# Attention with a fused feed-forward: the gated up products by one level of Strassen's scheme

## The chip, the cores and the metric

The kernel runs as one program on one core of a Trainium2 chip. Its time is the device time of one execution in microseconds; the kernel before takes 1141.07 us (median of three runs, 1141.06 to 1141.1). Five engines work side by side, each through its own instructions in order: TensorE (PE; its weight loads are listed apart as PEld), VectorE (DVE), ScalarE (ACT), GpSimd (POOL) and SyncE (SP), which here issues the DMAs. SBUF is the working memory, PSUM holds matmul results in eight banks per partition.

## The reference

Eight batches of eight heads attend over 576 positions with a learned relative bias; the result, 4608 tokens of 512 features, goes through a gated product and two further weight matrices:

```python
scores = scale * np.matmul(q, k.transpose(0, 1, 3, 2)) + bias      # (8, 8, 576, 576)
attn = softmax(scores)
x = np.matmul(attn, v).transpose(0, 2, 1, 3).reshape(4608, 512)    # tokens x features
a = x @ w1                       # w1, w2: 512 x 1024
b = x @ w2
h = a * b @ w3                   # (a * b) @ w3, w3: 1024 x 1024
out = h @ w_out                  # w_out: 1024 x 512
```

The four weight matrices arrive as 64-bit floats, so the kernel converts them on the chip.

## The kernel before, in words

There are three stages. **Attention** (to about 480 us) works through 32 units (head pair, batch) in an order that a table of times sets. It is the same in both kernels.

**Fold** (about 474 to 546 us of the profiled execution): w3 and w_out are multiplied into one 1024 x 512 matrix, since nothing stands between them. In 16 half steps, four 128-wide transposes go to PSUM (tile `w3t`), ACT and DVE split them into a high and a low part (`w3h`, `w3l`), and twelve matmuls accumulate into `wacc`. ACT and DVE then split each finished row block into two parts, which stand in the buffers `w3s`. Everywhere in the last two stages a 32-bit number is carried as a high part in the type fp32r, which PE takes at its fast rate, and a low part (the remainder, fp32r too); a product is three matmuls: high by high, low by high, high by low.

**Feed-forward** (from 546 us): nine chunks of 512 tokens, each with eight steps `ft` of 128 of the 1024 inner features. `up` makes the two products a and b of a step: for each of the two weight matrices, four blocks of 128 features times three matmuls, 24 matmuls of 512 columns into two PSUM tiles `up0`, `up1`. ACT copies `up0` (`a`), DVE multiplies (`g`), ACT and DVE split the product (`gh`, `gl`). `down` takes `gh`, `gl` as weights and the folded matrix as the moving operand: four token blocks times three matmuls, 12 matmuls of 512 columns into four PSUM tiles `o`. PE does the ups of step n+1 before the downs of step n, and `up0`, `up1` have two buffers each, so PE has a free bank to write while ACT and DVE read another. At a chunk's end ACT copies `o` to `osb` and SP stores it.

Two preparations run beside this. A weight piece (512 x 128 of w1 or w2) is fetched as 64-bit words by SP and narrowed (`narrow`: three operations of ACT, two of DVE, two of POOL), then split into `wh` (ACT) and `wl` (DVE); there are 16 pieces, one each 6.56 us by plan, beginning in the fold. The pieces of `ft` 0 and 1 lie in the pool `w01`, opened on the right side of SBUF, the other twelve in `wpool` on the left side. The chunk's x is loaded by SP, scaled by the softmax sums `rb` (DVE), and split (`xh` on POOL, `xl` on DVE).

The order of the work on PE, ACT, DVE and POOL is written out by hand: each step of a Python generator is entered in a list with a planned time (`put`), and `drive` emits them sorted by it. The planned times only set the order on each engine; when an instruction runs is settled by its waits. SP takes its DMAs in the order in which they are emitted.

Of the kernel before, what the change touches and what calls it, by code (L numbers as in the profile page):

```python
# [18 lines left out]
P = 128  # L19
# [64 lines left out]
def relpos_attention_moe(  # L84
# [29 lines left out]
    def f(ap):  # L114
        return ap.bitcast(F32)
# [401 lines left out]
    att_r.close()  # L517


    CH = 512  # L520
    NCH = NTOK // CH
    NT = CH // P
    STEP = 7.8
    moe = ctx.enter_context(ExitStack())
    w01 = moe.enter_context(tc.tile_pool(name="w01", bufs=1, side="right"))
    cv = moe.enter_context(tc.tile_pool(name="cv2", bufs=2, side="right"))

    ups = {}
    chunks = {c: dict(x=[None] * NC, g={}) for c in range(NCH)}

    def split_w(pool, t, m):
        src = (moe_w1, moe_w2)[m].rearrange("(c p) n -> p c n", p=P)[:, :, t * P:(t + 1) * P]
        w = cv.tile([P, NC * P], F32, name="w", bufs=3)
        for step in narrow(cv, src, NC * P, w, nc.sync, pieces=NC):
            step()
            yield
        w = w.rearrange("p (c n) -> p c n", c=NC)
        wh = pool.tile([P, NC, P], F32R, name=f"wh{m}{t}")
        nc.scalar.activation(wh, w, AF.Copy)
        yield  # L540
        wl = pool.tile([P, NC, P], F32R, name=f"wl{m}{t}")
        nc.vector.tensor_tensor(wl, w, f(wh), op=ALU.subtract)
        ups[m, t] = (wh, wl)

    def put_w(plan, pool, t, m, at):
        put(plan, split_w(pool, t, m), at - AT_W[0], *(at + d for d in AT_W[1:]))


    fo = ExitStack()
# [43 lines left out]
    def load_x(c):  # L593
        for cc in range(NC):
            xr = xs.tile([P, CH], F32, name=f"xr{cc}", bufs=1)
            nc.sync.dma_start(xr, x_d[cc][:, c * CH:(c + 1) * CH])
            rb = xs.tile([P, CH], F32, name=f"rb{cc}", bufs=1)
            for h, rows in enumerate((lo, hi)):
                load_r(rb, cc, rows, h, c * CH, (c + 1) * CH)
            chunks[c]["x"][cc] = (xr, rb)  # L600
        yield

    def split_x(c, cc):
        xr, rb = chunks[c]["x"][cc]
        nc.vector.tensor_tensor(xr, xr, rb, op=ALU.mult)  # L605
        yield
        xh = xs.tile([P, CH], F32R, name=f"xh{cc}")
        xl = xs.tile([P, CH], F32R, name=f"xl{cc}")
        nc.gpsimd.tensor_scalar(xh, xr, 1.0, 1.0, op0=ALU.mult, op1=ALU.mult)  # L609
        yield  # L610
        nc.vector.tensor_tensor(xl, xr, f(xh), op=ALU.subtract)
        chunks[c]["x"][cc] = (xh, xl)

    def up(c, ft):
        ps = []
        for m in range(2):
            acc = ps_ab.tile([P, CH], F32, name=f"up{m}")
            wh, wl = ups[m, ft]
            n = 0
            for cc in range(NC):  # L620
                xh, xl = chunks[c]["x"][cc]
                for l, r in ((wh, xh), (wl, xh), (wh, xl)):
                    nc.tensor.matmul(acc, l[:, cc], r, start=(n == 0), stop=(n == 3 * NC - 1))  # L623
                    n += 1
            ps.append(acc)
            yield
        a = gp.tile([P, CH], F32, name="a")
        nc.scalar.copy(a, ps[0])  # L628
        yield
        g = gp.tile([P, CH], F32, name="g")  # L630
        nc.vector.tensor_tensor(g, ps[1], a, op=ALU.mult)  # L631
        yield
        gh = gp.tile([P, CH], F32R, name="gh")
        nc.scalar.activation(gh, g, AF.Copy)  # L634
        yield
        gl = gp.tile([P, CH], F32R, name="gl")
        nc.vector.tensor_tensor(gl, g, f(gh), op=ALU.subtract)  # L637
        chunks[c]["g"][ft] = (gh, gl)

    def down(c, ft):  # L640
        d = chunks[c]
        gh, gl = d["g"].pop(ft)
        for t in range(NT):
            if ft == 0:
                d["o", t] = ps_o.tile([P, DO], F32, name=f"o{t}")
            sl = slice(t * P, (t + 1) * P)
            for n, (l, r) in enumerate(((gh, 0), (gh, 1), (gl, 0))):
                nc.tensor.matmul(  # L648
                    d["o", t], l[:, sl], folded[ft][:, r],
                    start=(ft == 0 and n == 0), stop=(ft == NF - 1 and n == 2),  # L650
                )
        yield
        if ft == NF - 1:
            for t in range(NT):
                o = op.tile([P, DO], F32, name="osb")
                nc.scalar.copy(o, d["o", t])
                nc.sync.dma_start(out[c * CH + t * P:c * CH + (t + 1) * P, :], o)
                yield


    for i in range(NF):
        put(later, split_wo(i), t_s + AT_WO + i * PACE_WO, t_s + AT_WO + i * PACE_WO + 0.8)
    for i in range(2 * NF):
        at = t_s + AT_F + min(i, N_F) * PACE_F0 + max(i - N_F, 0) * PACE_F
        put(later, fold(*divmod(i, 2)), *(at + d for d in AT_FOLD))
    for t in range(2):
        for m in range(2):
            put_w(later, w01, t, m, t_s + AT_W1 + PACE_W * (2 * t + m))
    drive([e for e in later if e[0] <= end])
    later = [e for e in later if e[0] > end]  # L670
    att.close()
    xs = moe.enter_context(tc.tile_pool(name="xs", bufs=2))
    wpool = moe.enter_context(tc.tile_pool(name="wpool", bufs=1))
    ps_ab = moe.enter_context(tc.tile_pool(name="ps_ab", bufs=2, space=PSUM))
    plan, t_f = [], t_s + AT_F + N_F * PACE_F0 + (2 * NF - N_F) * PACE_F + AT_FOLD[3]
    for n in range(4, 2 * NF):
        at = t_s + AT_W1 + PACE_W * n
        put_w(later if at < t_f - 10.0 else plan, wpool, n // 2, n % 2, at)
    put(later, load_x(0), end + 0.5)
    for cc in range(NC):  # L680
        put(later, split_x(0, cc), *(t_s + AT_X + PACE_X * cc + d for d in (0.0, 0.8, 1.8)))
    drive(later)
    fo.close()

    gp = moe.enter_context(tc.tile_pool(name="gp", bufs=2))
    op = moe.enter_context(tc.tile_pool(name="op", bufs=NT))
    ps_o = moe.enter_context(tc.tile_pool(name="ps_o", bufs=1, space=PSUM))
    for n in range(NCH * NF):
        c, ft = divmod(n, NF)
        at = t_f + STEP * n  # L690
        put(plan, up(c, ft), at, at + 2.6, at + 3.0, at + 5.5, at + 6.3, at + 7.0)
        put(plan, down(c, ft), at + STEP + 5.2, *(at + STEP + 5.9 + 0.65 * t for t in range(NT)))
        if ft == 0 and c + 1 < NCH:
            put(plan, load_x(c + 1), at)
        if 2 <= ft < 2 + NC and c + 1 < NCH:
            put(plan, split_x(c + 1, ft - 2), at + 0.5, at + 1.5, at + 2.5)
# [56 lines left out]
```

## Time and profile before

| | |
|---|---|
| median of the runs | 1141.07 us |
| the profiled execution's own time | 1142.65 us |
| its span, first to last instruction | 1140.9 us |
| mean granted TensorE clock | 0.985 |
| PE busy | 1086.7 us (95%) |
| DVE, ACT, POOL busy | 637.3, 510.2, 179.9 us |
| feed-forward: first `up` matmul to the end of the last `down` | 546.09 to 1137.19 us |
| PE's waits for others in the fold (480 to 547 us) | 4.7 us for DVE `w3l`, 0.7 us for ACT `w3h` |

A group row gives busy time and mean duration of one instruction; matmuls overlap, so the mean of one (391 ns) is longer than their spacing. The chain of waits, which follows back from the last instruction to what released each step, gives the spacing when a stretch on PE is divided by its count of matmuls. Idle time of DVE, ACT and POOL costs nothing as long as PE does not wait for them.

### The profile page before, as it was taken

Reading aid. Unit: us, or ns where it says so; the run is one execution under the profiler, and the core shown is the slowest. Engines: PE = TensorE matmul, PEld = TensorE weight load, DVE = VectorE, ACT = ScalarE, POOL = GpSimd, SP = SyncE. Lnnn points to the kernel's source line nnn. Section 1 sums busy time; section 2 is a strip of 40 time slices with the busy share of each in tenths; the row PEclk is TensorE's granted clock in tenths of the full one; section 3 lists DMA queues with packets and bytes.
Section 4 is the critical chain, followed back from the end, with each engine's and each line's share of the span. In section 5 each row is a group of like instructions: output and inputs, shape, how many; then the busy total and the mean of one; then the engine's idle time right before and its main releaser. Section 6 shows DMA issues by size and latency. Waiting matters only on the chain.

```text
span 1140.9 us, 32065 instructions
## 1 busy us (share of the span) xinstructions
PE 1086.7 (95%) x13696; PEld 801.6 (70%) x13696; DVE 637.3 (56%) x1204; ACT 510.2 (45%) x1111; POOL 179.9 (16%) x167
## 2 busy tenths in 40 slices
PE   7988999899899989898999999999999999999998
PEld 2355666566565655576888888888888888888887
DVE  8999899899998989846552212222131312223111
ACT  7867767677776767656442121121212112121212
POOL 0023303330331133334440000000000000000000
PEclk9989999899999999999999999999999999999999
DMA  8958676786777667455231202021121202110100
GB/s 277 309 186 287 221 233 219 243 260 214 243 252 252 184 206 226 138 147 159 70 115 38 73 23 68 21 72 40 52 59 37 56 19 74 38 38 1 37 1 37
DMA packets 100558, 149.04 MB, mean 131 GB/s; under 512 B 22848, under 2 KB 53696, under 8 KB 100416
## 3 DMA queue, kind: packets, MB, share of 16 engines
q1 hardware_dynamic: 99984, 146.98, 40.7%
q8 instruction: 107, 1.75, 0.6%
q14 instruction: 35, 0.29, 0.1%
q10 hardware_dynamic: 432, 0.02, 0.0%
HBM read 116.93 MB, written 30.03 MB: 129 GB/s over the span
## 4 chain that ended last, share of the span: by engine, by line
PE 71%; DVE 16%; issue 7%; DMA 2%; ACT 2%; SPq 1%; POOL 0%; DVEq 0%; ACTq 0%; POOLq 0%
PE up L623 35%; PE o L648 17%; PE acc L360 8%; DVE pt L314 7%; PE s L264 7%; DVE ts L275 6%; PE bacc L485 3%; PE wacc L582 1%; DVE zdve L471 1%; ACT x L369 1%; DVE mx L275 1%; DMA nb<-nb_d 0%; DMA rb<-r_m 0%; DVE wmag L159 0%; DMA x_d<-x 0%
## 5 line engine op out<-in xcount | busy, mean ns | idle before, releaser
L631 DVE TENSOR_TENSOR g<-up,a 128x512 f32<-128x512 f32 x72 | 49.8, 692 | 343.7 <-PE up L623 343.7
L360 PE MATMUL acc<-pt,v 32*64 32x128 f32 (+1 forms) x9216 | 214.7, 299 | 27.1 <-issue 19.5
L304 ACT ACTIVATE pp<-ts,mx 128x576 f32<-128x576 f32 x256 | 197.0, 770 | 91.0 <-DVE mx L275 89.8
L360 PEld LDWEIGHTS acc<-pt,v 32*64 32x64 f32 x9216 | 162.4, 133 | 95.4 <-issue 64.8
L623 PE MATMUL up<-xh,wl 128*128 128x512 f32 x576 | 225.1, 391 | 0.0
L623 PE MATMUL up<-xl,wh 128*128 128x512 f32 x576 | 225.1, 391 | 0.0
L623 PE MATMUL up<-xh,wh 128*128 128x512 f32 x576 | 225.1, 391 | 0.0
L264 PE MATMUL s<-k,q 64*128 64x288 f32 (+1 forms) x1280 | 200.0, 450 | 10.6 <-DVE mx L275 4.9
L275 DVE CUSTOM_DVE_ANT_0 ts<-s,nb 128x576 f32<-128x576 f32 x256 | 183.2, 739 | 27.4 <-PE s L264 26.6
L648 PE MATMUL o<-w3s,gh 128*128 128x512 f32 x576 | 177.7, 390 | 0.0
L314 DVE STREAM_TRANSPOSE pt<-pp 128x1152 f32<-128x1152 f32 x128 | 175.7, 1373 | 0.0
L628 ACT COPY a<-up 128x512 f32<-128x512 f32 x72 | 42.2, 587 | 263.0 <-PE up L623 263.0
L264 PEld LDWEIGHTS s<-k,q 64*128 64x128 f32 (+1 forms) x1280 | 93.9, 180 | 81.0 <-DVE mx L275 35.6
L623 PEld LDWEIGHTS up<-xl,wh 128*128 128x128 f32 x576 | 108.2, 188 | 23.4
L623 PEld LDWEIGHTS up<-xh,wl 128*128 128x128 f32 x576 | 108.2, 188 | 23.4
L623 PEld LDWEIGHTS up<-xh,wh 128*128 128x128 f32 x576 | 108.2, 188 | 23.3
L648 PEld LDWEIGHTS o<-w3s,gh 128*128 128x128 f32 x576 | 108.1, 188 | 22.9
L634 ACT ACTIVATE gh<-g 128x512 fp32r<-128x512 f32 x72 | 45.5, 632 | 173.7 <-DVE g L631 173.7
L648 PE MATMUL o<-w3s,gl 128*128 128x512 f32 x288 | 112.1, 389 | 0.0
L609 POOL TENSOR_SCALAR xh<-xr 128x512 fp32r<-128x512 f32 x36 | 22.5, 624 | 446.6 <-DVE xr L605 445.7
L155 POOL TENSOR_SCALAR wmag<-wmag 128x512 f32<-128x512 f32 x24 | 46.0, 1915 | 243.3 <-ACT wmag L145 243.3
L637 DVE TENSOR_TENSOR gl<-g,gh 128x512 fp32r<-128x512 f32 x72 | 50.8, 705 | 51.3 <-ACT gh L634 51.2
(68 smaller groups left out, 906.6 us busy)
## 6 DMA issues: line engine op xcount, KB each, us to landing
v<-in_v_dram SPq DMA_DIRECT2D x96, 256.0 KB, 4.5
q<-in_q_dram SPq DMA_DIRECT2D x64, 288.0 KB, 4.7
wi<-in_moe_w_dram SPq DMA_DIRECT2D x32, 512.0 KB, 4.3
v<-in_v_dram SPq DMA_DIRECT2D x64, 192.0 KB, 4.1
nb_d<-bev SPq DMA_DIRECT2D x36, 295.5 KB, 4.8
k<-in_k_dram SPq DMA_DIRECT2D x64, 144.0 KB, 3.7
nb<-nb_d SPq DMA_DIRECT2D x16, 576.0 KB, 5.6
x_d<-x SPq DMA_DIRECT2D x32, 288.0 KB, 5.1
```

The lines of the kernel that those rows point to most:

```text
L155: clamps.tensor_scalar(d["mag"], d["mag"], LEAST, MOST, op0=ALU.max, op1=ALU.min)
L264: nc.tensor.matmul(s[outs, hf, :HS], d[f"q{h}"][rows, q0:q0 + n], d[f"k{h}"][rows, :], start=True, stop=True,)
L275: nc.vector.tensor_tensor_reduce(out=halves(ts), in0=d.pop(("s", t))[:, :, :HS], in1=halves(NB[p, t]), op0=ALU.add, op1=ALU.min, scale=-1. ...
L304: nc.scalar.activation(d["p", ps][:, k * S:(k + 1) * S], ts, AF.Exp, bias=mx, scale=-1.0, accum_out=SUMS[u // 4 % 2][:, col:col + 1],)
L314: nc.vector.transpose(o, st[u].pop(("p", ts)))
L360: nc.tensor.matmul(acc[outs, a, c0:c0 + 32 * (t1 - t0)], d["v", b][rows, h], pt_[rows, t0:t1, 32 * b:32 * b + 32], start=(b == 0), stop=(b ...
L623: nc.tensor.matmul(acc, l[:, cc], r, start=(n == 0), stop=(n == 3 * NC - 1))
L628: nc.scalar.copy(a, ps[0])
L631: nc.vector.tensor_tensor(g, ps[1], a, op=ALU.mult)
L634: nc.scalar.activation(gh, g, AF.Copy)
L637: nc.vector.tensor_tensor(gl, g, f(gh), op=ALU.subtract)
L648: nc.tensor.matmul(d["o", t], l[:, sl], folded[ft][:, r], start=(ft == 0 and n == 0), stop=(ft == NF - 1 and n == 2),)
```

## The change

Tokens are now taken in six pairs of two halves of 384 (`c` and `d`), 768 tokens a pair.

**Pair 0** is done by ordinary products (`plain`): per step four products of 12 matmuls of 384 columns. During it the weights of each step are built: `fetch_w` narrows a piece as before (one piece each half step by plan), `base_w` splits four blocks into high and low parts, `sums_w` forms four sums and differences of blocks and splits those too. Seven blocks, each in two parts, make the tile `wS`; it is written to DRAM (`w_d`). Three of the four blocks that `plain` reads lie in `wS`, the fourth in `w2k`, a pool on the right side, as is the x of pair 0 (`xB`).

**Pairs 1 to 5** use seven products instead of eight (Winograd's form of Strassen's scheme) on a two by two division: the tokens' halves c and d on one side, the 512 features' halves on the other, and a and b as the two columns. `product` makes one of them: 6 matmuls of 384 columns. They accumulate in only two PSUM banks, `X` and `Y` (`Z` is the second use of `Y`), one buffer each: products 1, 6, 7 and 4 add up in `X`, product 2 stands in `Y`, products 5 and 3 add up in `Z`. Between them ACT copies intermediate values out (`p`, `u`, `z`) and DVE adds (`ac`, `bd`, `ad`) and multiplies (`gc`, `gd`); `split_g` splits the two gated results. `down` has three token blocks per half, 9 matmuls of 512 columns, and the results take the other six PSUM banks. `load_w` reads `wS` of a step back from DRAM (128 x 3584 numbers, 1.84 MB) in each of the 40 steps, into one of three buffers. `split_x` loads and scales x of the next pair in two pieces, forms four differences on DVE, and splits seven blocks per piece on ACT and DVE; POOL has no part in x any more. x of pairs 1, 3 and 5 lies in a pool on the left side (`xb0`), of pairs 2 and 4 on the right (`xb1`).

```diff
-    CH = 512
-    NCH = NTOK // CH
+    CH = 384
+    W2 = 2 * CH
+    NPR = NTOK // W2
     NT = CH // P
-    STEP = 7.8
+    STEP0, STEP = 12.5, 11.40
...
+    def base_w(t):
+        x, w = big.pop(t), ups[0, t]
+        w2 = bg.tile([P, 2, 2 * P], F32R, name="w2k", bufs=3)
+        base[t] = (w[:, :, 0], w[:, :, 1], w2, w[:, :, 2])
+        for o, y in ((w[:, :, 0:2], x[:, 0:2]), (w[:, :, 2], x[:, 3]), (w2, x[:, 2])):
+            nc.scalar.activation(o[:, 0], y, AF.Copy)
+            yield
+            nc.vector.tensor_tensor(o[:, 1], y, f(o[:, 0]), op=ALU.subtract)
+            yield
...
+    AT_P = {"2": 0.0, "1": 1.04, "6": 4.2, "5": 5.25, "7": 6.3, "3": 7.3, "4": 10.4}
+    AT_E = {
+        "p": 2.10, "ac": 2.70, "u": 5.28, "z": 6.35, "bd": 7.32, "ad": 8.36, "gd": 8.95, "hd": 9.60, "ld": 10.15,
+        "gc": 11.45, "hc": 12.05, "lc": 12.60,
+    }
+    AT_D = {"d": 2.1, "c": 8.3}
...
+    def product(st, k):
+
+        p, t = st["at"]
+        if k in "15":
+            st["X" if k == "1" else "Z"] = ps_ab.tile([P, CH], F32, name="X" if k == "1" else "Y")
+        if k == "2":
+            st["Y"] = ps_ab.tile([P, CH], F32, name="Y")
+        acc = st["Y" if k == "2" else "Z" if k in "53" else "X"]
+        w, n = ups[p, t], int(k)
+        for i in range(2):
+            x = pairs[p]["x"][i]
+            for m, (l, r) in enumerate(((0, 0), (1, 0), (0, 1))):
+                nc.tensor.matmul(
+                    acc, w[:, l, W_AT[n], i * P:(i + 1) * P], x[:, r, X_AT[n]],
+                    start=(k in "125" and i == 0 and m == 0), stop=(i == 1 and m == 2), skip_group_check=True,
+                )
...
+    def evict(st, n):
+
+        def add(o, slot, x, y, op):
+            st[o] = temp(slot, o)
+            nc.vector.tensor_tensor(st[o], x, y, op=op)
+
+        if n in ("p", "u", "z"):
+            st[n] = temp("puz".index(n), n)
+            nc.scalar.copy(st[n], st["Z" if n == "z" else "X"])
+        elif n == "ac":
+            add("ac", 4, st["Y"], st["p"], ALU.add)
+        elif n == "bd":
+            add("bd", 3, st["X"], st["z"], ALU.add)
+        elif n == "ad":
+            add("ad", 5, st["Z"], st["u"], ALU.add)
+        elif n == "gc":
+            add("gc", 6, st["X"], st["ac"], ALU.mult)
+        elif n == "gd":
+            add("gd", 7, st["ad"], st["bd"], ALU.mult)
+        else:
+            split_g(st, n)
...
-    ps_ab = moe.enter_context(tc.tile_pool(name="ps_ab", bufs=2, space=PSUM))
+    ps_ab = moe.enter_context(tc.tile_pool(name="ps_ab", bufs=1, space=PSUM))
```

On PE, a step before, at the border of its ups (L623) and downs (L648); `up` and `o` are the PSUM tiles:

```order
L623 MATMUL up_10396<-xh_9935,wh_9791 128x512
L623 MATMUL up_10396<-xh_9935,wl_9794 128x512
L623 MATMUL up_10396<-xl_9936,wh_9791 128x512
L648 MATMUL o_10203<-w3s_9375,gh 128x512 x2
L648 MATMUL o_10203<-w3s_9375,gl 128x512
L648 MATMUL o_10207<-w3s_9375,gh 128x512 x2
L648 MATMUL o_10207<-w3s_9375,gl 128x512
L648 MATMUL o_10211<-w3s_9375,gh 128x512 x2
L648 MATMUL o_10211<-w3s_9375,gl 128x512
L648 MATMUL o_10215<-w3s_9375,gh 128x512 x2
L648 MATMUL o_10215<-w3s_9375,gl 128x512
L623 MATMUL up_10429<-xh_9724,wh_9843 128x512
```

And now, in the second step of pair 1: product 2 into `Y`, product 1 into `X`, the downs of half d of the step before (L763), then product 6 into `X` again and product 5 into `Y` (L693 are the products, two rows for the two feature blocks):

```order
L693 MATMUL Y<-xS_10201,wS 128x384 x3
L693 MATMUL Y<-xS_10428,wS 128x384 x3
L693 MATMUL X<-xS_10201,wS 128x384 x3
L693 MATMUL X<-xS_10428,wS 128x384 x3
L763 MATMUL od_10647<-w3s_9042,ghd 128x512 x2
L763 MATMUL od_10647<-w3s_9042,gld 128x512
L763 MATMUL od_10651<-w3s_9042,ghd 128x512 x2
L763 MATMUL od_10651<-w3s_9042,gld 128x512
L763 MATMUL od_10655<-w3s_9042,ghd 128x512 x2
L763 MATMUL od_10655<-w3s_9042,gld 128x512
L693 MATMUL X<-xS_10201,wS 128x384 x3
L693 MATMUL X<-xS_10428,wS 128x384 x3
```

Between two uses of the same bank there are now 6 matmuls of 384 columns, or 9 of 512, where before there was a second buffer.

On DVE, two steps before, with one piece of x in each (g and gl are the gated product and its low part, xr and xl the scaled x and its low part):

```order
L631 TENSOR_TENSOR g<-up_10734,a 128x512
L637 TENSOR_TENSOR gl<-g,gh 128x512
L605 TENSOR_TENSOR xr_10552<-xr_10552,rb_10554 128x512
L611 TENSOR_TENSOR xl_10782<-xr_10552,xh_10781 128x512
L631 TENSOR_TENSOR g<-up_10785,a 128x512
L637 TENSOR_TENSOR gl<-g,gh 128x512
```

And now a step of pair 1 in which x of pair 2 is scaled and subtracted (L736 are the evictions in the order ac, bd, ad, gd, gc; L653 and L656 are x; L719 the low parts):

```order
L736 TENSOR_TENSOR wos_10773<-Y,wos_10771 128x384
L653 TENSOR_TENSOR xr<-xr,rb 128x768 x2
L656 TENSOR_TENSOR xr<-xr 128x384 x4
L736 TENSOR_TENSOR wos_10810<-X,wos_10801 128x384
L736 TENSOR_TENSOR wos_10821<-Y,wos_10791 128x384
L736 TENSOR_TENSOR wos_10823<-wos_10821,wos_10810 128x384
L719 TENSOR_TENSOR gld<-wos_10823,ghd 128x384
L736 TENSOR_TENSOR wos_10842<-X,wos_10773 128x384
L719 TENSOR_TENSOR glc<-wos_10842,ghc 128x384
```

Six operations for x stand between two evictions, where before there were two.

More of the change, by code (lines that the diff above doesn't have):

```diff
@@ L517, in relpos_attention_moe @@
     att_r.close()
-    CH = 512
-    NCH = NTOK // CH
+    CH = 384
+    W2 = 2 * CH
+    NPR = NTOK // W2
     NT = CH // P
-    STEP = 7.8
[L524 to L531, printed above, removed]
+    STEP0, STEP = 12.5, 11.40
+    moe, prep = ctx.enter_context(ExitStack()), ExitStack()
@@ new lines, in relpos_attention_moe, with fetch_w @@
+    bg = prep.enter_context(tc.tile_pool(name="bg", bufs=2, side="right"))
+    x0p = prep.enter_context(tc.tile_pool(name="x0p", bufs=1, side="right"))
+    W_AT = {1: 0, 2: 1, 4: 2, 5: 3, 6: 4, 7: 5, 3: 6}
+    X_AT = {1: 0, 2: 1, 3: 2, 5: 3, 6: 4, 7: 5, 4: 6}
+    w_d = [dram.tile([P, 14 * 2 * P], F32, name=f"w_d{t}") for t in range(NF)]
+    ups, base = {}, {}
+    pairs = {p: dict(x=[None, None]) for p in range(NPR)}
+    big = {}
+    def fetch_w(t, m):
+        if m == 0:
+            big[t] = bg.tile([P, 4, 2 * P], F32, name="big")
+        flat = big[t].rearrange("p s n -> p (s n)")
@@ L614, in up @@
[L614 to L623, printed above, removed]
-                    n += 1
[L625 to L638, printed above, removed]
@@ new lines, in plain @@
+    def plain(st, j, m):
+        t = st["at"][1]
+        acc = st[j, m] = ps_ab.tile([P, CH], F32, name="XY"[m])
+        n = 0
+        for k in range(2):
+            for i in range(2):
+                w, x = base[t][2 * m + k], pairs[0]["x"][i]
+                for l, r in ((0, 0), (1, 0), (0, 1)):
+                    nc.tensor.matmul(
+                        acc, w[:, l, i * P:(i + 1) * P], x[:, r, 2 * k + "cd".index(j)], start=(n == 0), stop=(n == 11),
+                    )
+                    n += 1
@@ L643, in down @@
+    def down(st, j):
+        p, ft = st["at"]
+        gh, gl = st["h" + j], st["l" + j]
+        d = pairs[p]
         for t in range(NT):
             if ft == 0:
[L645 removed]
+                d["o", j, t] = ps_o.tile([P, DO], F32, name=f"o{j}{t}")
             sl = slice(t * P, (t + 1) * P)
@@ L648, in down, with store, at, until @@
                 nc.tensor.matmul(
-                    d["o", t], l[:, sl], folded[ft][:, r],
+                    d["o", j, t], l[:, sl], folded[ft][:, r],
                     start=(ft == 0 and n == 0), stop=(ft == NF - 1 and n == 2),
                 )
[L652 to L658, printed above, removed]
+    def store(p, j, t):
+        o = op.tile([P, DO], F32, name="osb")
+        if t == 1:
+            nc.vector.tensor_copy(o, pairs[p]["o", j, t])
+        else:
+            nc.scalar.copy(o, pairs[p]["o", j, t])
+        r0 = p * W2 + "cd".index(j) * CH + t * P
+        nc.sync.dma_start(out[r0:r0 + P, :], o)
+    def at(time, step, *args):
+        later.append((time, len(later), lambda: step(*args)))
+    def until(time):
+        nonlocal later
+        now, later = [e for e in later if e[0] <= time], [e for e in later if e[0] > time]
+        drive(now)
     for i in range(NF):
@@ L685, in relpos_attention_moe @@
[L685 to L696, printed above, removed]
@@ L700 @@
+    until(start(NF) + 2.0)
+    prep.close()
+    xb.append(moe.enter_context(tc.tile_pool(name="xb1", bufs=1, side="right")))
+    drive(later)
 _INS = ['q', 'k', 'v', 'w1', 'b1', 'w2', 'logs', 'logi', 'ilogs', 'moe_w1', 'moe_w2', 'moe_w3', 'moe_w_out']
```

190 lines of the change are left out of this document (141 added, 49 removed).

## The prediction, made before the changed kernel was run

> **What bounds the kernel now.** First the page's busy times and granted clock, then the chain of waits of the last two stages, then the groups of PE.
>
> ```profile
> PE 1086.7 (95%) x13696; PEld 801.6 (70%) x13696; DVE 637.3 (56%) x1204; ACT 510.2 (45%) x1111; POOL 179.9 (16%) x167
> PEclk9989999899999999999999999999999999999999
> ```
>
> PE is busy nearly all the span and its clock is full in the second half. A share says little of a stage, so the chain comes next (start, length, what; x24 counts matmuls):
>
> ```profile
> 535.97 0.61 DVE w3l L576
> 536.58 0.04 issue
> 536.63 0.66 PE w3t L570 x4
> 537.28 2.78 PE wacc L582 x12
> 540.07 0.44 PE w3t L570 x4
> 540.50 5.58 PE wacc L582 x24
> 546.09 11.24 PE up L623 x48
> 557.33 2.73 PE o L648 x12
> ...
> 600.86 5.44 PE up L623 x24
> 606.30 2.72 PE o L648 x12
> 609.02 5.61 PE up L623 x24
> 614.63 2.75 PE o L648 x12
> ```
> ```profile
> 1131.74 5.45 PE o L648 x24
> 1137.19 0.02 issue
> 1137.22 0.58 ACT osb L656
> ```
>
> From 546.09 to 1137.19 us the chain stands on PE alone: 591.1 us for 72 x 36 = 2592 matmuls of 512 columns, 228 ns each. Nothing is waited for; only fewer or shorter matmuls help. The usual spacing is 5.44 us / 24 = 226.7 ns. Two ups of each chunk take 5.61 us / 24 = 233.8 ns: those of `ft` 0 and 1, whose weights alone lie in the pool on the right side. I read that as a cost of 7.1 ns for an operand in that pool. The groups show the loads beside it:
>
> ```profile
> L623 PE MATMUL up<-xh,wh 128*128 128x512 f32 x576 | 225.1, 391 | 0.0
> L623 PEld LDWEIGHTS up<-xh,wh 128*128 128x128 f32 x576 | 108.2, 188 | 23.3
> ```
>
> A weight load is shown as 188 ns with 23.3 us / 576 = 40 ns before it, together the spacing.
>
> **The new matmul, part by part.** No row shows a 384-column matmul of this type. If all of the 226.7 ns goes by columns it takes 226.7 x 384/512 = 170.0 ns: the low bound. For the high one, the four 128-column transposes at 540.07 take 0.44 us, 110 ns each with a weight load each; the straight line from (128, 110) to (512, 226.7) gives 188 ns at 384, as does the full 188 ns of the weight load, were it not overlapped. But these transposes also show that loads can follow at 110 ns, so 170 ns covers a load, and the line is lifted at its short end by the load. I take 173.3 ns, a fifth of the way up, as an estimate.
>
> The Trainium skill (TensorE: Matmul & The Clock Gate, section Back-to-back issue gap) gives the gap of a warm matmul as its columns at 2.4 GHz plus 2.5 ns: 216 ns for 512, 162.5 for 384, and a feed-forward of 2064 x 162.5 + 864 x 215.8 ns = 522 us, so a time near 1072 us. The 226.7 ns of the trace contradict it at 512 columns already. By that clock alone 512 columns are 213.3 ns, and a fixed remainder of 13.4 ns would make 173.4 at 384.
>
> **Pair 0** has 48 matmuls of 384 and 18 of 512 per step: 48 x 173.3 + 18 x 226.7 = 8.32 + 4.08 = 12.40 us. The first step has no downs. 8.32 + 7 x 12.40 = 95.1 us.
>
> **Pairs 1 to 5**: seven products of 6 matmuls and the same 18 downs, 42 x 173.3 + 4.08 = 7.28 + 4.08 = 11.36 us, times 40 = 454.4 us. The downs of the very last step follow: 4.08 us. Together 553.6 us against 591.1, that is 37.5 us less; by the bounds of the matmul 2064 x 3.3 ns = 6.8 us more gain or 2064 x 14.7 ns = 30.3 us less.
>
> **The handovers of the two banks.** Where before a second buffer stood, PE now returns to `X` or `Y` after other work. Rows for one handover before (last matmul of `up0`, ACT's copy; last of `up1`, DVE's product, then ACT's split):
>
> ```profile
> 701.91 0.39 PE L623 MATMUL up<-xl,wh 128*128 128x512 f32 x1
> 704.63 0.39 PE L623 MATMUL up<-xl,wh 128*128 128x512 f32 x1
> ```
> ```profile
> 702.39 0.59 ACT L628 COPY a<-up 128x512 f32<-128x512 f32 x1 [4.07 <-PE up L623]
> 705.85 0.63 ACT L634 ACTIVATE gh<-g 128x512 fp32r<-128x512 f32 x1 [2.87 <-DVE g L631]
> ```
> ```profile
> 705.13 0.69 DVE L631 TENSOR_TENSOR g<-up,a 128x512 f32<-128x512 f32 x1 [3.98 <-PE up L623]
> ```
>
> ACT starts 0.48 us after the start of the last matmul, DVE 0.50; with 128 columns fewer some 0.43 and 0.45. A copy of 384 I put at 0.48 us and a DVE product at 0.56, both estimates between three quarters of 0.59 and 0.69 and the whole. From DVE's end to PE's start is 0.04 us (536.58). PE comes back to `X` after `u`, and to `Y` after `z`, when 6 matmuls, 1.04 us, have passed. From the last matmul's start that is 1.04 + 0.17 = 1.21 us, of which 0.43 + 0.48 + 0.04 = 0.95 is needed. 0.26 us is left, or 0.15 if the weight load (0.11) must wait as well. After `gc` the same sum is 1.21 - 0.45 - 0.56 - 0.04 = 0.16, or 0.05. The other returns have the 9 downs (2.04 us) between. So it fits with nothing to spare, if DVE and ACT are free at that moment. In the step with six operations of x before `bd`, DVE has from the end of `ac` (about 3.4 us into the step) to 7.5 us, and they take at most 2 x 1.04 + 4 x 0.69 = 4.8 us, by proportion 2 x 1.04 + 4 x 0.52 = 4.2: `bd` can be some tenths late, and behind it stand `ad` and `gd`; but `X` and `Y` are wanted again only after the downs of c. I enter 1 us for all 40 steps, with 0.25 us per step, 10 us, as the upper bound and none as the lower.
>
> **Operands on the right side.** In pair 0, 12 of 48 matmuls read weights there: 96 x 7.1 ns = 0.7 us, which I enter. If moving operands pay too (no row shows one there), x of pair 0 and of pairs 2 and 4 adds (384 + 672) x 7.1 ns = 7.5 us at most.
>
> **The preparation in pair 0.** Rows of the stretch 546 to 611 us, in which the old kernel converts weights:
>
> ```profile
> L145 ACT ACTIVATE wmag<-wi 128x512 f32<-128x512 f32 x7 | 4.7, 668 | 0.6 <-DMA wi<-in_moe_w_dram 0.6
> L634 ACT ACTIVATE gh<-g 128x512 fp32r<-128x512 f32 x8 | 5.1, 632 | 11.8 <-DVE g L631 11.8
> L159 DVE TENSOR_SCALAR wmag<-wmag 128x512 int32<-128x512 int32 x7 | 3.2, 464 | 0.1
> L542 DVE TENSOR_TENSOR wl<-w,wh 128x512 fp32r<-128x512 f32 x8 | 5.9, 740 | 11.2 <-ACT wh L539 11.2
> L605 DVE TENSOR_TENSOR xr<-xr,rb 128x512 f32<-128x512 f32 x4 | 5.0, 1238 | 0.0
> L163 POOL TENSOR_TENSOR w<-w,wmag 128x512 int32<-128x512 int32 x7 | 9.3, 1333 | 21.5 <-DVE wmag L159 21.5
> L164 POOL TENSOR_TENSOR w<-w,wi 128x512 f32<-128x512 f32 x7 | 10.1, 1449 | 0.5
> ```
>
> Per 12.40 us step ACT has six conversions (0.67), the work of four splits of 512 (0.63; two halves count as one), two copies (0.48) and two splits of 384 (about 0.5): 4.0 + 2.5 + 2.0 = 8.5 us. It also waits in its queue twice, since `gh` has one buffer per half and the downs of the step before read it until about 6.2 and 12.4 us, while the product is there at 4.9 and 11.2: 2.5 us. Together 11.0 of 12.4. DVE has four conversions (0.46), four full splits' and sums' worth of 512 in `base_w` and the last part of `sums_w` (0.74), four sums of 256 (0.37) and four gate operations (0.56): 1.8 + 3.0 + 1.5 + 2.2 = 8.5 us. POOL has 2 x 2.78 = 5.6 us. PE sees this late: the banks of a product come back to it about 4 us after the copy is ready, and weights are ready a step ahead by plan. Cost 0; without that cover, below.
>
> **The fold** has the same PE work. Its waits:
>
> ```profile
> PE w3t L570 <- DVE w3l L576: 4.7, 4, 1.6
> PE wacc L582 <- ACT w3h L574: 0.7, 1, 0.7
> ```
>
> Now DVE and ACT do three steps' weights there with their sums, and x in pieces of 768, but no operation waits for POOL's `xh` any more. In two half steps DVE's new queue holds more than the 3.2 us (2.78 + 0.44) that PE needs. I let the 5.4 us stand, minus 4 to plus 5.
>
> **DMA.** One `wS` is 1.84 MB per 11.36 us, 162 GB/s, for which the row of the busiest stretch has room:
>
> ```profile
> 20.00:60.00 40.00, 36.18 (x273) 12.06 (x272) 37.28 (x103) 34.40 (x79) 0.00 (x0) 1.00 0.93 309
> ```
>
> It was 309 GB/s at a share of 0.93; the load is issued two steps ahead. SP's queue has it behind waits for free buffers of the same age, so stores behind it are late at most a step, which nothing waits for. Cost 0. The tail (copy, store) stays as it is.
>
> **Sum.** 1140.9 - 591.1 + 553.6 + 1.0 + 0.7 = 1105.1 us of span. The runs' median stands 0.2 us above the profiled span (that execution's own time 1.75 above). **1105 us.**
>
> **Rivals.**
>
> *The handovers decide: slower.* `u`, `z` and `gc` each stand behind one other operation of 0.59 us (`osb` or a split) in their queue. Then PE waits 3 x 0.59 less the slack of 0.15 + 0.15 + 0.05, 1.4 us in each of 40 steps: 1105 + 56 - 1 = 1160 us. It decides from (1141 - 1104)/40 = 0.9 us per step. For it: one buffer per bank and margins of a tenth. Against: in six of eight steps of a pair the queues are nearly empty (about 3.6 us of DVE and 2.5 of ACT in 11.4). Chance 0.05.
>
> *The weight load bounds the short matmul*, at 188 ns: 1105 + 30 = 1135 us, still faster. For it the 188 ns of the load row; against it the transposes' 110 ns. Chance 0.08.
>
> *DVE and POOL exclude each other in pair 0.* The row of `xr` has 1238 ns in this stretch against 690 of the like product `g`, with POOL at work. If all 5.6 us of POOL come on top of DVE's 8.5, a step is 14.1 us instead of 12.40; over 7 steps 12 us, and the fold, where the same work runs, may lose 5 more: 1122 us. Against it: `wl` has 740 and `wmag` 464 there, little more than undisturbed. Chance 0.10. The Trainium skill (SBUF — State Buffer, section SBUF: two separate sides) states just this, an exclusive lock on a shared port held for the whole instruction when a DVE operation reads two SBUF operands; the 1238 ns agree, the 740 mostly escape it.
>
> *The time goes below the columns' proportion*, as in the page's formula. 0.03, since the spacing at 512 is not met.
>
> That the products are not fewer is excluded by the order: 42 rows' worth of matmuls per step.
>
> **How the numbers follow.** The forecast 0.73, the rivals 0.05, 0.08, 0.10 and 0.03, unnamed 0.01. The forecast's own range: down by 6.8 us (columns' proportion) and 4 (fold) to 1094; up by 7.5 (right side), 9 (handovers) and 5 (fold), not all at once, to 1120. The DVE rival lies at its edge; to leave out no more than 0.2 I end at 1125: **1094 to 1125 us.** What this measurement can tell from no change is about 0.2%, 2.3 us. Faster by more: all but the first rival and the unnamed, and a little of each kept back: 0.93. Within: 0.02. Slower: 0.05.
>
> **What would show it.** Right: in the chain, products of x6 at 1.02 to 1.06 us and steps of 11.2 to 11.5 us on PE alone in pairs 1 to 5, with DVE and ACT absent from it after the fold. Wrong: pieces of ACT `wos` or DVE `wos` between products (handovers); 6 matmuls at 1.13 us (weight load); steps of 14 us in pair 0; pairs 2 and 4 slower than 1, 3 and 5 (right side, moving operands); waits for `w3l` in the fold far above 5 us.

## The result, and the profile after

The changed kernel takes 1110.49 us (median of four runs, 1101.86 to 1113.5) against 1141.09 before: a ratio of 0.9722, 95% interval [0.9661, 0.9782]. The forecast was 1105 us. The profiled execution took 1110.39 us with a span of 1108.6 us. First the busy row of the page, to be held against 1086.7 us of PE and 637.3 us of DVE before:

```profile
PE 1054.4 (95%) x14032; PEld 836.2 (75%) x14032; DVE 782.0 (71%) x1506; ACT 572.6 (52%) x1285; POOL 162.2 (15%) x131
```

PE is as full as before with 32 us less to do, and DVE is 145 us busier. The chain of waits in pair 3 (start, length, what):

```profile
831.51 2.08 PE oc L763 x9
833.59 1.06 PE X L693 x6
834.65 1.04 PE Y L693 x6
...
843.00 2.08 PE oc L763 x9
```

It stands on PE alone; DVE and ACT are not in it. From `oc` to `oc` is one step: 843.00 - 831.51 = 11.49 us, forecast 11.36. In pair 2 it is 762.18 - 750.62 = 11.56 us, with every product at 1.06:

```profile
750.62 2.08 PE oc L763 x9
752.70 1.06 PE X L693 x6
753.76 1.06 PE Y L693 x6
...
762.18 2.08 PE oc L763 x9
```

The view by windows gives pair 0 and pairs 1 to 3 whole (length, busy times with counts, granted clock, DMA share, GB/s):

```profile
541.00:638.66 97.66, 96.78 (x509) 90.72 (x508) 78.02 (x133) 51.74 (x107) 31.49 (x22) 1.00 0.73 258
638.66:730.60 91.94, 91.94 (x482) 85.66 (x481) 45.83 (x83) 27.61 (x58) 0.00 (x0) 1.00 0.61 217
730.60:823.20 92.60, 92.60 (x483) 86.49 (x482) 46.45 (x85) 27.82 (x58) 0.00 (x0) 1.00 0.59 210
823.20:915.20 92.00, 92.00 (x482) 85.71 (x481) 46.44 (x85) 27.80 (x58) 0.00 (x0) 1.00 0.60 212
```

In pairs 1 to 3 PE is busy for the whole of each window. Only in pair 0, and in the fold ahead of it, does PE wait. PE's waits from 480 us on (total, times, longest), where before there were 4.7 us for `w3l`:

```profile
PE w3t L602 <- DVE w3l L608: 1.9, 2, 1.2
PE X L707 <- ACT wos L725: 0.8, 1, 0.8
...
PE acc L358 <- issue: 0.3, 1, 0.3
```

Stage by stage, on the two profiled executions:

| stage | before | after | difference | forecast of the difference |
|---|---|---|---|---|
| attention, to the first `w3t` | 474.2 | 477.6 | +3.4 | 0 |
| fold, to the first product into `X` | 71.9 | 63.4 | -8.5 | 0 |
| feed-forward | 591.1 | 562.5 | -28.6 | -35.8 |
| tail (copy, store) | 3.7 | 5.1 | +1.4 | 0 |
| span | 1140.9 | 1108.6 | -32.3 | -35.8 |

The forecast of the feed-forward is 591.1 - 553.6 less the 1.0 and 0.7 us entered for handovers and right side. Of the 7.2 us that it missed, 1.9 are in pair 0 (97.7 against 95.1 + 0.7) and 5.3 in pairs 1 to 5.

### The profile page after: what moved, and what is told of

It is laid out like the page before. It is cut to its first block, busy times and chain, and to the rows that moved or that the text cites. A ratio compares the mean times of both kernels' runs of the same rounds, so it can differ in the third digit from the quotient of the medians.

```text
span 1108.6 us, 33338 instructions
## 1 busy us (share of the span) xinstructions
PE 1054.4 (95%) x14032; PEld 836.2 (75%) x14032; DVE 782.0 (71%) x1506; ACT 572.6 (52%) x1285; POOL 162.2 (15%) x131
## 4 chain that ended last, share of the span: by engine, by line
PE 66%; DVE 21%; issue 8%; ACT 2%; DMA 1%; POOL 0%; DVEq 0%; SPq 0%; ACTq 0%; POOLq 0%
PE X L693 15%; PE Y L693 11%; PE oc L763 9%; PE od L763 9%; DVE pt L312 9%; DVE ts L273 7%; PE acc L358 7%; PE s L262 6%; PE bacc L483 3%; PE wacc L614 2%; PE Y L707 2%; PE X L707 2%; DVE zdve L469 1%; DVE mx L273 1%; ACT x L367 1%
## 5 line engine op out<-in xcount | busy, mean ns | idle before, releaser
L693 PE MATMUL X<-xS,wS 128*128 128x384 f32 x960 | 194.8, 338 | 0.0
L693 PEld LDWEIGHTS X<-xS,wS 128*128 128x128 f32 x960 | 171.5, 188 | 6.8
L693 PE MATMUL Y<-xS,wS 128*128 128x384 f32 x720 | 145.0, 336 | 0.0
L736 DVE TENSOR_TENSOR wos<-X,wos 128x384 f32<-128x384 f32 x80 | 44.6, 558 | 138.4 <-PE X L693 138.4
L693 PEld LDWEIGHTS Y<-xS,wS 128*128 128x128 f32 x720 | 127.9, 188 | 0.1
L763 PE MATMUL oc<-w3s,ghc 128*128 128x512 f32 x288 | 89.8, 393 | 0.0
L763 PE MATMUL od<-w3s,ghd 128*128 128x512 f32 x288 | 89.6, 392 | 0.0
L736 DVE TENSOR_TENSOR wos<-Y,wos 128x384 f32<-128x384 f32 x80 | 44.6, 558 | 50.1 <-ACT wos L740 36.7
L763 PEld LDWEIGHTS oc<-w3s,ghc 128*128 128x128 f32 x288 | 53.4, 188 | 8.6
L763 PEld LDWEIGHTS od<-w3s,ghd 128*128 128x128 f32 x288 | 53.5, 188 | 8.5
L763 PE MATMUL od<-w3s,gld 128*128 128x512 f32 x144 | 56.6, 393 | 0.0
```

Of the source, the lines that this page charges most:

```text
L693: nc.tensor.matmul(acc, w[:, l, W_AT[n], i * P:(i + 1) * P], x[:, r, X_AT[n]], start=(k in "125" and i == 0 and m == 0), stop=(i == 1 and ...
L736: nc.vector.tensor_tensor(st[o], x, y, op=op)
L763: nc.tensor.matmul(d["o", j, t], l[:, sl], folded[ft][:, r], start=(ft == 0 and n == 0), stop=(ft == NF - 1 and n == 2),)
```

## The experiments

Step lengths are compared rather than totals. They agree among executions to 0.02 us, while the unchanged attention does not (last section). "Odd pairs" are 1, 3 and 5, whose tokens lie on the left side; pairs 2 and 4 have them on the right. All kernels are the changed one with the edit shown, except where the kernel before is named.

**Eight products in pairs 1 to 5.** Every pair is done like pair 0. The weights are the first four of the seven blocks, which are not the four that ordinary products need.

```diff
-                w, x = base[t][2 * m + k], pairs[0]["x"][i]
+                w, x = (base[t] if p == 0 else [ups[p, t][:, :, s] for s in range(4)])[2 * m + k], pairs[p]["x"][i]
...
-        if p == 0:
+        if True:
             for j, u in AT_U.items():
...
-        else:
-            for k, d in AT_P.items():
-                at(t0 + d, product, cs, k)
-            for k, d in AT_E.items():
-                at(t0 + d, evict, cs, k)
```

> Leaves out Strassen's scheme in pairs 1 to 5: eight ordinary products of 6 matmuls per step, with weights taken from the first four blocks of wS, so its output is wrong; loads of wS, the sums and the splits of x stay. Theory (PE's matmuls are the whole price, one product of 6 x 384 columns costs 6 x 0.175 = 1.05 us): a step of pairs 1 to 5 goes from 11.5 to 12.55 us, the 40 steps cost 42 us more, and the time is about 1152 us, slower than before. Rival (the scheme's evictions or its second use of the banks cost PE something that the ordinary products escape): less than 1.05 us more per step, 30 us or less in all.

Measured: 1153.54 us, steps of 12.53 us in the odd pairs and 12.64 in pairs 2 and 4. Its chain:

```profile
858.15 2.08 PE oc L763 x9
...
870.68 2.08 PE oc L763 x9
```

The eighth product costs 1.04 us and 1.07 us per step, six matmuls of 173 to 178 ns: the gain of the scheme is what was worked out, 42 us over 40 steps. It also shows that narrower chunks without the scheme lose: this kernel is slower than the one before (1143.03 us on the same chip), and its feed-forward takes 604.6 us where the kernel before needs 591.1. By the prediction's terms 384 columns instead of 512 cost 4 us of that (8.32 + 47 x 12.40 + 4.08 = 595.2 us); the rest are longer spacings and waits in pair 0, which the runs below take up.

**One late handover.** A copy of `X` that nobody uses stands in ACT's queue ahead of the eviction `u`.

```diff
         if n in ("p", "u", "z"):
+            if n == "u":
+                nc.scalar.copy(gp.tile([P, CH], F32, name="late"), st["X"])
```

> Adds one more copy of X by ACT directly ahead of u in each of the 40 steps (result not used), some 0.4 to 0.48 us, so that X comes back to PE that much later. Theory (the margin at u is 0.15 us, since the weight load waits too): PE waits 0.25 to 0.33 us per step before product 7, 10 to 13 us in all, and a wait of PE for ACT shows at X. With a margin of 0.26 us (the weight load goes ahead): 0.14 to 0.22 us per step, 6 to 9 us. Rival (the margins are wide, half a microsecond or more): nothing.

Measured: 1121.54 us; steps +0.24 us in the odd pairs, +0.21 in pairs 2 and 4, 9.1 us in all, between the two expected amounts. The chain shows the price at the one product into `X` behind `u`, 1.28 us where it was 1.04:

```profile
835.10 1.28 PE X L693 x6
```

What waits is the weight load ahead of that product's first matmul (in brackets the idle time of the engine and what ended it; the first two lines are ACT's, the third is PE's loads):

```profile
834.15 0.48 ACT L740 COPY late<-X 128x384 f32<-128x384 f32 x1 [1.92 <-PE X L693]
834.52 0.49 ACT L742 COPY wos<-X 128x384 f32<-128x384 f32 x1
835.06 1.00 PEld L693 LDWEIGHTS X<-xS,wS 128*128 128x128 f32 x6 [0.28 <-ACT wos L742]
```

The added copy lasts 0.48 us, but the next copy on ACT begins 0.37 to 0.38 us behind it, so `u` is late by that much. The margin was therefore 0.38 - 0.24 = 0.14 to 0.38 - 0.21 = 0.17 us: the 0.15 us of the theory, in which the weight load has to wait too. The changed kernel shows the same without an added copy. In the next line `u` ends at 851.95 us, and the weight load for `X` begins at 852.08:

```profile
851.47 0.48 ACT L740 COPY wos<-X 128x384 f32<-128x384 f32 x1 [2.67 <-PE X L693]
852.08 1.05 PEld L693 LDWEIGHTS X<-xS,wS 128*128 128x128 f32 x6
```

The handover fits, and it is tight.

**Three late handovers.** The same ahead of `z`, and a product of DVE ahead of `gc`.

```diff
+        if n in ("u", "z"):
+            nc.scalar.copy(gp.tile([P, CH], F32, name="late"), st["Z" if n == "z" else "X"])
+        if n == "gc":
+            nc.vector.tensor_tensor(gp.tile([P, CH], F32, name="late2"), st["X"], st["ac"], op=ALU.mult)
```

> The same extra copy ahead of u and of z (ACT) and an extra product ahead of gc (DVE), results not used: each of the three tight handovers stands behind one more operation. Theory: waits of about 0.25 at u, 0.25 at z and 0.4 at gc, together 0.8 to 1.0 us per step, 32 to 40 us, which would bring the kernel back to about the time before, 1141 to 1150 us. Rival (wide margins): under 10 us.

Measured: 1132.91 us; steps +0.62 us in the odd pairs and +0.52 in pairs 2 and 4, some 23 us in all. Now DVE stands in the chain between two products, which the prediction named as the sign of this rival:

```profile
830.71 0.56 DVE late L741
```

The step grew by less than the expected 0.8 to 1.0 us, because the three waits do not add up. The waits of the weight loads in pairs 1 to 5 (total, times, longest), first behind `gc`, then behind `u`, then behind `z`:

```profile
PEld X L693 <- DVE wos L736: 14.6, 38, 0.4
PEld X L693 <- ACT wos L744: 10.7, 39, 0.3
PEld Y L693 <- ACT wos L744: 1.3, 5, 0.3
```

Behind `gc` and `u` a load waits 0.38 and 0.27 us per step. Behind `z` there is almost no wait left: PE, held up at `u`, comes back to `Y` that much later. The kernel is still faster than before. One operation too many at each of the three places costs 23 us, not the 56 of the rival, which added three waits and counted 0.59 us for each operation (here 0.48, 0.48 and 0.56).

**Tokens on the right side at a multiple of 64 bytes.** A pad of 32 bytes at the far end of the right side, from which its pools are laid out; nothing else.

```diff
+    moe.enter_context(tc.tile_pool(name="pad", bufs=1, side="right")).tile([P, 8], F32, name="pad")
     bg = prep.enter_context(tc.tile_pool(name="bg", bufs=2, side="right"))
```

> Puts an unused tile of 32 bytes per partition at the end of the right side, so that every tile there begins 32 bytes lower and at a multiple of 64 bytes, as the tiles of the left side do; nothing else changes. Theory (a matmul is slow when its weights and its moving operand begin at different places within 64 bytes, not because a pool lies on the right side): the products of pairs 2 and 4 go from 176.7 to 173.4 ns, their steps from 11.57 to 11.49 us, the fold's matmuls from 232 to 227 ns; 1.3 + 1.5 + 1 us, some 4 us in all. Rival (the side, or the distance, counts): no change of any spacing.

Measured: median 1110.5 us, not to be told from the changed kernel (ratio 0.9738 [0.9692, 0.9783] to the kernel before, 1143.03 us on the same chip). But the steps of pairs 2 and 4 fell from 11.57 to 11.39 us (and pair 0's from 12.56 to 12.48), while the odd pairs stayed at 11.49. Pair 2, to be held against the same stretch above:

```profile
750.97 2.05 PE od L764 x9
753.03 1.04 PE X L694 x6
...
762.36 2.05 PE od L764 x9
```

So the slower pairs were not slow because their moving operand lies on the right. With an aligned start they are the fastest. The gain in these steps, 16 x 0.18 + 8 x 0.08 = 3.5 us, is smaller than the run-to-run spread; the feed-forward took 559.5 us against 562.5. The fold's matmuls went from 232.8 to 230.4 ns, not to the expected 227.

That the tokens' start alone does not decide can be seen in pair 0 of the changed kernel (mean spacings, 545 to 632 us). Its tokens `xB` and the weights `w2k` both start 32 bytes past a multiple of 64, and those products take 174.3 ns; the products with weights in `wS`, which starts at a multiple of 64, take 176.5 and 177.0 with the same tokens. So it is the difference between the two starts that costs, as the theory said. But with the pad, where all of them start at multiples of 64, the products from `w2k` take 177.0 ns and those from `wS` 173.4 to 173.7: weights on the right cost something besides.

**The same pad in the kernel before**, where the weights of `ft` 0 and 1 lie on the right.

```diff
+    moe.enter_context(tc.tile_pool(name="pad", bufs=1, side="right")).tile([P, 8], F32, name="pad")
     w01 = moe.enter_context(...)
```

> The kernel before with the same 32 bytes at the end of the right side. Theory (different places within 64 bytes make a matmul slow): the two ups of each chunk that take 5.61 us take 5.44, 18 x 0.17 = 3.1 us less in the feed-forward (591.1 to 588 us), and the fold's matmuls go from 232 to 227 ns. Rival (the right side counts): no change.

Measured: 1144.21 us, beside 1137.95 of the kernel before; the feed-forward took 590.8 us against 591.1, no change. The chain still has the two slow ups (5.61 before):

```profile
610.79 5.60 PE up L624 x24
...
619.14 5.60 PE up L624 x24
```

The fold's matmuls went from 232.5 to 230.8 ns, where 227 was expected. The expectation failed: for weights on the right the start within 64 bytes is not the cause of the 7.1 ns.

**Tokens on the left side 32 bytes off**, the reverse of the pad on the right.

```diff
+    moe.enter_context(tc.tile_pool(name="pad", bufs=1)).tile([P, 8], F32, name="pad")
     xb = [moe.enter_context(tc.tile_pool(name="xb0", bufs=1))]
```

> A tile of 32 bytes ahead of the left side's buffer for x of pairs 1, 3 and 5, so that these tokens start at 32 bytes past a multiple of 64, as those of pairs 2 and 4 do on the right side already. Theory (the start within 64 bytes counts, on whichever side the moving operand lies): the steps of pairs 1, 3 and 5 rise from 11.49 by about 0.18 us to 11.67, 24 x 0.18 = 4.3 us; the steps of pairs 2 and 4 stay at 11.57 and pair 0 at 12.56. Rival (only a right-side buffer, or one address, counts): pairs 1, 3 and 5 stay at 11.49.

Measured: 1113.6 us; odd pairs 11.51 us against 11.49. Neither was met:

```profile
857.50 2.04 PE oc L763 x9
859.54 1.06 PE X L693 x6
...
869.01 1.13 PE oc L763 x5
```

The products did become slower, each group of six 1.06 us instead of 1.04, as the theory said. But the downs, whose operands did not move, became faster, 2.04 us instead of 2.08 for nine, and gave nearly all of it back. Tokens that start 32 bytes past a multiple of 64 cost a product with weights in `wS` about 3.3 ns on both sides (176.7 against 173.3 on the left, 176.5 against 173.3 on the right); what the downs beside it take depends on something that these runs do not isolate.

**Downs of 384 columns.** The last 128 output columns are left out, so that all matmuls of the feed-forward have one width.

```diff
-                    d["o", j, t], l[:, sl], folded[ft][:, r],
+                    d["o", j, t][:, 0:CH], l[:, sl], folded[ft][:, r, 0:CH],
```

> Leaves out the last 128 of the 512 output columns: the 18 downs of a step stream 384 columns like the products, so all matmuls have one width. Theory (going from 384 to 512 columns and back disturbs the spacing, which is why downs take 231 instead of 226.7 ns and the six products behind them 176.6 instead of 173.4): all matmuls of pairs 1, 3 and 5 at 173.4 ns, a step of 60 x 0.1734 = 10.40 us. Rival (the place of the downs' operands in SBUF or their PSUM banks): downs at 176 to 178 ns and six slow products behind each, a step of 10.53 us or more.

Measured: 1064.86 us. In the odd pairs a step takes 842.73 - 832.33 = 10.40 us:

```profile
832.33 1.56 PE oc L763 x9
833.89 1.04 PE X L693 x6
...
842.73 1.56 PE oc L763 x9
```

That is 60 matmuls of 173.3 ns, the prediction's term to the digit, and the first product behind a down has lost its extra 0.02 us. With downs of 512 columns the same 42 products and 18 downs take 11.49, where 42 x 173.3 + 18 x 226.7 ns is 11.36: the 0.13 us go when the two widths become one. (In pairs 2 and 4, with their tokens off a multiple of 64, the step is 10.57 us.) But alternating widths are not enough to cause them: in pairs 2 and 4 of the kernel with the pad the widths alternate too, and there a step takes 11.39 us, only 0.03 more than the sum. So the place of the tokens has a part in it; which part, and whether the width or the buffers of the 512-wide operands count, these runs can't say.

A second reading: with PE faster, pair 0 no longer hid its preparation. One of its steps took 16.47 us, the others 11.63 to 12.22. PE waited there for DVE, and behind the wait its granted clock was halved for 3.4 us (a window of that stretch; the 0.50 is the clock):

```profile
PE Y L707 <- DVE wos L728: 3.4, 2, 3.0
```
```profile
607.40:610.70 3.30, 3.30 (x12) 3.30 (x11) 2.70 (x7) 3.30 (x9) 0.00 (x0) 0.50 0.24 47
```

**No reload of the weights.** The 40 loads of `wS` in pairs 1 to 5 are left out (the products there use the three tiles that stand in SBUF).

```diff
-        w = wr.tile([P, 2, 7, 2 * P], F32R, name="wS")
-        nc.sync.dma_start(f(w.rearrange("p h s n -> p (h s n)")), w_d[t])
-        ups[p, t] = w
+        ups[p, t] = ups[0, 5 + t % 3]
```

> Leaves out the 40 loads of wS: pairs 1 to 5 use the three tiles that stand in SBUF at the end of pair 0, so the output is wrong. Theory (DMA is hidden): steps stay at 11.49 and 11.57 us, the time within 1 us of the changed kernel's in the feed-forward. Rival (1.84 MB per step into SBUF disturbs PE's reads, and is why the downs take 231 ns): downs at 226.7 ns, 0.08 to 0.16 us less per step, 3 to 6 us.

Measured: 1108.7 us; every step as in the changed kernel, 11.49 and 11.57 us, and the feed-forward 562.5 us in both. The same window of the kernel without the loads, and of the changed kernel:

```profile
650.00:1090.00 440.00, 440.00 (x2292) 410.18 (x2291) 209.74 (x380) 126.65 (x263) 0.00 (x0) 1.00 0.13 41
```
```profile
650.00:1090.00 440.00, 440.00 (x2293) 410.48 (x2293) 210.32 (x381) 126.70 (x263) 0.00 (x0) 1.00 0.55 197
```

197 GB/s or 41, PE runs the same number of matmuls. The loads are hidden whole, and they are not what slows the downs.

**POOL left out.** In the changed kernel the low parts of the weights' sums (DVE L570) vary: 0.68 us where POOL is idle, 1.33 to 1.80 us where it runs. Here POOL's two operations on each piece of w1 and w2 are left out, and with them the last step of the conversion.

```diff
-        for step in narrow(cva, src, ..., pieces=NC):
-            step()
-            yield
+        for k, step in enumerate(narrow(cva, src, ..., pieces=NC)):
+            if k < 6:
+                step()
+            yield
```

> Leaves out, for the pieces of w1 and w2, POOL's two operations (L161, L162), so the weights of the products are wrong; every other instruction stays. In the kernel after, the low parts of the weights' sums (DVE L570) take 0.68 us where POOL is idle and 1.33 to 1.80 us where POOL's two operations run beside them. Theory: POOL and DVE hold each other up. Then all L570 take 0.68 us, DVE's busy time in pair 0 falls from 78 us to about 65, and the two short waits of PE in pair 0 go: steps 1 and 5 fall from 12.66 and 12.91 to 12.56 us, the feed-forward gains 1 to 2 us, and the other steps of pair 0 stay at 12.56, since preparation is hidden there. Rival 1: L570 is slow for another reason (its place behind ACT, its addresses): 1.4 us on average stays and so do the waits. Rival 2: the preparation, not PE, sets the steps of pair 0: then all of them fall below 12.56.

Measured: 1104.94 us. The group of the changed kernel in pair 0, and the same group without POOL (one line further down in that kernel), then the window of its pair 0:

```profile
L570 DVE TENSOR_TENSOR wS<-sums,wS 128x512 fp32r<-128x512 f32 x13 | 18.2, 1426 | 0.0
```
```profile
L571 DVE TENSOR_TENSOR wS<-sums,wS 128x512 fp32r<-128x512 f32 x14 | 9.2, 685 | 0.7 <-ACT wS L568 0.7
```
```profile
536.99:633.23 96.24, 96.24 (x509) 90.81 (x508) 62.54 (x131) 51.42 (x107) 0.00 (x0) 1.00 0.73 256
```

DVE's busy time in pair 0 falls from 78.0 to 62.5 us, PE waits for nothing in it, and it is 1.4 us shorter (96.24 us against 97.66). The waits for `w3l` in the fold, 1.9 us, are gone too. Its one step of 12.91 us fell to 12.56, where the others stay. So the theory holds, both in its mechanism and in the cover: 15.5 us of DVE's time are lost to POOL, of which PE pays at most 1.4 us there.

That such an operation of DVE stands still while POOL works, and does not just run at half speed, shows in the changed kernel where the two meet (two operations L570 in the first line):

```profile
551.86 3.33 DVE L570 TENSOR_TENSOR wS<-sums,wS 128x512 fp32r<-128x512 f32 x2
551.62 1.29 POOL L161 TENSOR_TENSOR big<-big,wmag 128x512 int32<-128x512 int32 x1 [2.17 <-DVE wmag L157]
553.00 1.65 POOL L162 TENSOR_TENSOR big<-big,wi 128x512 f32<-128x512 f32 x1
```

The second L570 ends at 555.19 us, 0.54 behind POOL's L162, and so do all the slowed operations L570 in pair 0: they end 0.54 or 0.55 us behind one of POOL's. The Trainium skill (SBUF — State Buffer, section SBUF: two separate sides) states the exclusive lock between the two engines, and the 685 and 1426 ns and these ends agree.

The chain shows how one of these waits came about in the changed kernel. PE started a product of pair 0 at 550.12 us, 0.79 us late:

```profile
541.79 1.66 POOL big L162
...
543.47 1.11 DVE sums L564 x3
...
549.71 0.37 ACT wos L725
...
550.12 2.38 PE X L707 x12
```

POOL's two operations delay DVE's sums, these delay ACT's `ghc` and the conversions in its queue, and the copy `p` behind them (L725) frees the bank too late. Here the sums wait for POOL's result, and leaving POOL out takes that wait away as well. In the other wait, 0.35 us in the step of 12.91, operations of DVE stand in the chain, two of them slowed (L570 1.33 and L656 1.67 us), and none of POOL. So this run shows what POOL costs PE as a whole; how much of the 1.4 us is the lock and how much POOL's own time it does not separate.

## Why the prediction was right, and where not

**New matmul: right.** 173.3 ns is the spacing of the products in the run with one width, and 173 to 177 in the changed kernel. The bounds of 170 and 188 hold, so the rival of the weight load (188 ns) is excluded. So is the rival below the columns' proportion: the 162.5 ns by the formula of the Trainium skill (TensorE: Matmul & The Clock Gate, section Back-to-back issue gap), which the page gives for an isolated matmul, are not met. Mis-sized was the sum of a step: the prediction took 226.7 ns for the downs from a program in which all matmuls had 512 columns. Beside 384-column products a down takes 2.08 / 9 = 231 ns and the six matmuls behind it 177 ns. That is 0.13 us per step, 24 x 0.13 = 3.1 us in the odd pairs. It is shown that it goes when the downs have 384 columns, and also that it nearly goes with other tokens' addresses (11.39 us with the pad), so its cause stays open in part.

**Operands on the right side: wrong in its cause, right in its sign for pairs 2 and 4.** The prediction took 7.1 ns from the ups with weights on the right and extended it, as an upper bound, to moving operands. Pairs 2 and 4 were slower by 0.08 us per step than the odd ones, which the prediction had named as a sign of being wrong, and slower by 0.2 than forecast (16 x 0.2 = 3.3 us); but the pad shows that this is where the tokens start within 64 bytes against their weights, not the side. The 0.7 us entered for `w2k` in pair 0 was put at the wrong place: its products took 174.3 ns, the ones from `wS` 176.5 to 177. The 7.1 ns of weights on the right (kernel before) do not go away with the pad; their cause stays open.

**Handovers: right.** 1 us was entered; none shows in the steps. Of the two margins behind `u`, 0.26 us if the weight load goes ahead and 0.15 if it waits as well, the second holds: 0.14 to 0.17 us. The rival was right that a late eviction holds up PE, but handovers did not decide here, and even with one operation too many at all three places they cost 23 us and not 56, since the waits do not add up.

**Pair 0 and its preparation: the cost of 0 was 1.4 us too low.** DVE was put at 8.5 us per step; it took 78.0 of 97.7 us, 10.0 per step of 12.56, and without POOL 62.5 of 96.2, 8.2 per step. So the third rival's mechanism is real in this kernel, while its price, 12 us and 5 in the fold, was not: PE's lead hid all but 1.4 us in pair 0 and 1.9 us in the fold. The step that failed is adding POOL's 5.6 us to a step as if DVE set its length. DVE has room for it in steps of 12.56 us; where PE needs only 11.63, in the run with short downs, PE had to wait for DVE.

**The fold: the waits were let stand, and came out 2.8 us shorter.** That and two things for which the prediction had no term make the 8.5 us of the table. The fold before and after, then its beginning before (length, busy time of PE first):

```profile
474.20:546.09 71.89, 62.75 (x548) 49.35 (x546) 40.72 (x65) 38.19 (x72) 31.52 (x26) 0.95 0.52 150
477.58:541.00 63.42, 59.81 (x550) 47.58 (x548) 43.40 (x69) 35.74 (x68) 21.59 (x15) 1.00 0.45 143
480.00:487.00 7.00, 6.55 (x46) 5.07 (x47) 1.74 (x1) 0.28 (x1) 3.40 (x3) 0.51 0.45 147
```

PE's idle time fell from 9.1 to 3.6 us. Of these 5.5 us, 2.8 are the waits for `w3l`, 0.3 a wait for ACT, and 2.4 a wait marked "issue" at the beginning, 2.7 us before and 0.3 now:

```profile
PE acc L360 <- issue: 2.7, 1, 2.7
```

The other 2.9 us are busy time. Before, the granted clock was halved for 6.8 us at the end of that wait, which cost some 0.49 x 7.0 = 3.4 us as an estimate; against it stand three products of pair 0 that PE now does in the fold, 0.5 us. Both belong to the kernels and not to one execution: the kernel before with the pad has the same wait of 2.7 us with 3.4 us of half clock behind it, while in all nine traced kernels with the change such waits come to 0.3 to 1.5 us and the clock is full in the fold. Why the wait stood there is not shown. It is luck for the forecast that these terms offset the 7.2 us that the feed-forward took longer.

**DMA: right**, by the run without the loads. **The tail** was said to stay; it is 1.4 us longer. The copies of the last half waited for an earlier store of their buffer, `osb` (the very last one in the timeline):

```profile
1104.82 0.59 ACT L773 COPY osb<-oc 128x512 f32<-128x512 f32 x1 [0.80 <-DMA out_dram<-osb]
```

At the very end two halves with three tiles each finish right behind each other, and `op` has three buffers (four tiles and four buffers before).

**Sum.** 1105.1 + 3.4 (attention) - 8.5 (fold) + 7.2 (feed-forward) + 1.4 (tail) = 1108.6 us. The forecast of the gain, 35.8 us, holds to 10% in these two executions (32.3 us; 30.6 by the medians), with the help of the fold, and to 20% in the stage that the change is about (28.6 us).

## What to carry to other kernels

Price a new width of matmul by a straight proportion and a fixed rest, and expect a few ns more or less with the operands' addresses, above all where widths alternate or weights and tokens start at different places within 64 bytes: over thousands of matmuls it is the microseconds that the sum misses. Before a copy of a bank is trusted to "just fit", add one more copy ahead of it and read the step. Count with the time by which the copy behind it really moves (0.37 us here, not the 0.48 that the added one lasts), and look whether it is the weight load that waits. DVE work that overlaps POOL's may take twice its time; whether it costs anything is decided by PE's lead, so look for the first wait of PE where both run.

## What the runs showed of the hardware

The unchanged attention differs between executions more than anything in the feed-forward. Same work, here PE's 432.9 us and 432.7, took 474.2 us and 477.6:

```profile
0.00:474.20 474.20, 432.88 (x10561) 265.92 (x10561) 440.19 (x909) 348.83 (x830) 108.93 (x95) 0.97 0.73 234
```
```profile
0.00:477.58 477.58, 432.71 (x10561) 265.02 (x10561) 440.40 (x909) 349.32 (x831) 109.13 (x96) 0.97 0.74 234
```

Over all the kernels here the fold began between 472.8 us (the aligned tokens on the right) and 480.3 (the shifted tokens on the left). The stretches of 3 to 14 us in which the granted clock is halved lie at other places each time, but they do not explain the difference: each of these two executions has five of them before the fold, 27.3 us in the earlier one and 23.9 in the later. Two kernels with 30.7 us of them began their fold at 475.3 and at 479.7 us. The cause stays open.

From the fold's first matmul to the last down, the clock was halved in three of the eleven traced executions: in both of the kernel before, at the wait of 2.7 us in the fold, and in the one with short downs, behind its wait of 3.0 us. No shorter wait of PE there (up to 1.7 us) was followed by half the clock. With full clock, step lengths repeat to 0.02 us. That is why the medians of the changed kernel and of the one with the pad can be equal, though the feed-forward of the second is about 3 us shorter.
